# Split-fp32 matmuls of the last stage with weights standing for two of three token groups, and four places where operands, evictions, stores and loads change engine or order

## The chip, the cores and the metric

The kernel runs on one core of one Trainium2 chip. The metric is the device time of one launch in microseconds (us); 829.38 is the median of three runs of the kernel before (828.85 to 832.74). TensorE (PE) multiplies, VectorE (DVE) and ScalarE (ACT) do elementwise work, GpSimd (POOL) does a little of it and issues the accumulating transfers, SyncE (SP) issues all other transfers.

## The reference

Windowed causal attention, a gated layer with SiLU, and a second, ungated pair of layers, all in fp32 on 2304 tokens of width 512:

```
attention: B=4, H=8, S=576, D=64, window 64, softmax, then heads side by side -> x [2304, 512]
moe:  x = (silu(x @ w_gate) * (x @ w_val)) @ w_out          512 -> 1536 -> 512
moe2: out = ((x @ w1) * (x @ w2)) @ w3 @ w_out2             512 -> 1024 -> 1024 -> 512
```

## The kernel before

**Two words.** Each fp32 operand is held as a high and a low word in the format that TensorE takes. The high word is a rounded copy made by a cast (`cast`, line 218, ScalarE); the low word is the difference (`rest`, line 227, VectorE). A product takes three passes: high by high, high by low, low by high (`PASSES`).

**Seven products.** Every large product is a 2x2 block product with seven multiplications instead of eight (`PRODUCTS = (1, 2, 5, 6, 7, 4, 3)`). For the moving tokens this needs, besides the raw blocks, sums and differences of them (`combine`, line 231). An operand of product p and contraction block m has a name that ends in `pm`: `hf0_42` is the operand of product 4, block 2, of token group 0.

**Two ways to a low word.** Normally VectorE subtracts. In a few cases ScalarE writes the negated high word and an accumulating transfer of POOL's queue adds the source to it (`gather`, lines 234 to 236). Line 358 is that ScalarE instruction for the first gated stage; `RESTS` says for which products of which token group this is done there.

**Stages.** Tokens run in three groups of 768 (`TP`), each as two halves of 384 (`T`). Attention comes first and fills other engines' time with the first operands. Then come the first gated stage (`gated`, matmuls at line 666, results added up at lines 678 to 693, h stored by SP at line 756), the projection back to width 512 (`project`, line 830, evicted by ScalarE for one token half and VectorE for the other), the second gated stage with the same function, and the final part (`final`). In the final part w3 @ w_out2 is first multiplied into one matrix w34 (`row`, line 988, out of tiles z and w3T that SP loads at lines 862 and 874). Then the three token groups are multiplied with it (`Group`, line 1008, matmuls at line 1054). `begin` puts the loads of z and w3T into the plan during the second gated stage.

**The last stage before.** The tokens stand: a 128 x 128 piece of the operand hf is the weight, 256 columns of w34 move. A product is 3 pieces of 128 tokens x 4 blocks x 3 passes = 36 matmuls for each half of the tokens of a group, so 7 x 36 = 252 in a group. Results lie in PSUM with tokens on partitions. ScalarE copies 128 x 256 (line 1024), VectorE adds 128 x 256 (line 1028), SP stores rows of 512 or 256 columns (line 1034).

**What sets the order.** A planner at build time (`Plan`, lines 92 to 164) keeps a list of jobs with an assumed cost for every engine and hands them out as its own clock goes on (`advance`). `need` forces a job out directly before the instruction that uses it. On the chip each engine runs its instructions strictly in the order so fixed: an instruction that waits holds all behind it on its engine.

Of the kernel before, what the change touches and what calls it, by code (L numbers as in the profile page):

```python
# [37 lines left out]
def window_attention_moe_kernel(ctx: ExitStack, tc: tile.TileContext, q, k, v, w_gate, w_val, w_out, w1, w2, w3, w_out2, out):  # L38
# [286 lines left out]
    class Operands:  # L325
# [2 lines left out]

        def __init__(self, x, name, after=None, by_dma=(), rest_by_dma=(), due=0.0):
            self.ops, self.jobs = {}, {}

            at = {1: (0, 0), 2: (1, 0), 5: (0, 0), 6: (0, 0), 7: (0, 1), 4: (1, 0), 3: (1, 1)}
            sums = {5: ((0, 1), (1,)), 6: ((1, 1), (5,)), 7: ((1, 1), (5,)), 4: ((0, 0), (6, 2))}

            def blk(m, r, c):
                return x[2 * r + m]()[:, T * c:T * c + T]

            last = {}  # L340
            for p in PRODUCTS:
                for m in range(2):
                    wait, when = [after[p]] if after else [], due + AT[p]
# [12 lines left out]
                    if p in rest_by_dma:  # L356
# [278 lines left out]
    def gated(xop, left, order, func, hd, events, apart=0):  # L635


        hs = {}
        behind, xs = [], []

        def later(n, fn):
# [12 lines left out]
        class Unit:  # L654
# [49 lines left out]
            def product(self, p):  # L704
# [19 lines left out]
                elif p == 6:  # L724
                    plan.wait(self.read)
                    self.mm(self.al, 6)
                    self.c12 = self.own(0, 1, "c12")
                    self.copy(self.c12, self.al)
                elif p == 7:
                    plan.wait(self.read)  # L730
                    self.mm(self.al, 7)
                    c22 = self.own(1, 1, "c22")
                    self.copy(c22, self.al)

                    def summed():
                        self.summed = self.add(c22, c22, self.be)
                        if self.x:
                            self.put(1, 1, c22)
                        else:
                            later(2, lambda: self.put(1, 1, c22))  # L740
                    later(1, summed)
                elif p == 4:
                    plan.wait(self.read)
                    self.mm(self.al, 4)
                    self.put(1, 0, self.al)
                elif p == 3:
                    plan.wait(self.summed)
                    self.mm(self.be, 3)
                    self.add(self.c12, self.c12, self.be)
                    if self.x:  # L750
                        self.put(0, 1, self.c12)
                    else:
                        later(2, lambda: self.put(0, 1, self.c12))
                    if self.x:
                        for i, t in enumerate(hs.pop((self.fp, self.tp))):
                            nc.sync.dma_start(out=hd[self.fp, self.tp][:, i, :], in_=t)
# [45 lines left out]
    def project(rows, wos, events):  # L802

        NF, NM = DF // P, DM // P
        for tp in range(NTP):
# [42 lines left out]
    def final(rows):  # L848
# [9 lines left out]
        def queue_z(f):  # L858
            for x in range(2):
                def load(eng, x=x):  # L860
                    zt[f, x] = slot([P, DM], F32R, f"z{f}{'hl'[x]}")
                    eng.dma_start(out=zt[f, x].bitcast(F32), in_=zd[f][:, x, :])
                jobs["z", f, x] = loading(load, (), 1)

        def queue_w3(n):

# [2 lines left out]
            for g in range(0, NI, 3):  # L869
# [6 lines left out]

                def word(x, g=g, k=k):
                    return w3T[i][g // 3][:, x, :k * P]
                a = loading(load, [done[n - 3]] if n > 2 else (), 1)
# [55 lines left out]
        class Left:  # L935


            def __init__(self, tp):
# [17 lines left out]
                for p in PRODUCTS:  # L956
                    for m in range(R):
# [11 lines left out]
                        b = rest(lambda m=m, p=p: self.ops[p, m][:, 1], lambda m=m, p=p: blk(m, *at[p]),  # L969
                                 lambda m=m, p=p: self.ops[p, m][:, 0], [a], T)  # L970
# [25 lines left out]
            plan.slots += 3  # L996

        def begin():
            keep, plan.rank = plan.rank, -1
            queue_w3(0)  # L1000
            queue_w3(1)
            for f in range(NI):
                queue_z(f)
            for n in range(2, NI):
                queue_w3(n)
            plan.rank = keep

        class Group:
# [28 lines left out]
            def product(self, p):  # L1037
# [12 lines left out]
                for t in range(3):  # L1050
# [24 lines left out]
                        self.store(1, t, 0 if self.tp == NTP - 1 else None)  # L1075
                    plan.advance(1.44)

        def run():
            for n in range(NI):
                if n == 3:  # L1080
# [195 lines left out]

    def operands(tp):
        xop1[tp] = Operands([lambda c=c: X[tp, c] for c in range(KC)], f"xo{tp}",
                            {p: written[m] for p, m in WRITTEN[tp].items()} if tp in WRITTEN else None, BY_DMA[tp], RESTS[tp], 14.0 * tp)

    LANDING = {2: 11.2, 3: 8.5, 7: 6.0}
    second = {4: mark(), 8: mark()}
# [96 lines left out]
```

## Time and profile before

| | us |
|---|---|
| median of three runs | 829.38 |
| profiled execution | 830.3 |
| its span in the trace | 828.6 |
| TensorE busy in the span | 815.5 |
| VectorE / ScalarE / GpSimd busy | 633.0 / 455.7 / 78.2 |

The span runs from the first to the last recorded instruction; 1.7 us of the profiled execution lie around it. The granted TensorE clock is at the upper level in the whole span. A busy time is the union of the engine's instructions, so neighbours that overlap in a pipeline are counted once; mean durations are therefore longer than the distance between two starts.

### The profile page before, as it was taken

To read this page: it belongs to the slowest core of one execution; us is meant where nothing else is said; L and a number is where in the kernel's file an instruction comes from. 1 tells how busy PE (TensorE), PEld (TensorE's weight loads), DVE (VectorE), ACT (ScalarE), POOL (GpSimd) and SP (SyncE) were. 2 spreads that over 40 slices of the span, in tenths; PEclk is the share of its full clock that TensorE was granted. 3 is DMA by queue.
4 is the path that set the end of the run, shared out by engine and by line. 5 is a ranking of instruction groups with operands and counts; after the bars stand their busy time and mean duration, and the time that the engine had idled before them with its cause. 6 is when DMAs were issued, how large, how long until landed. Compare 5 with 4: busy or idle time off the path is not lost.

```text
span 828.6 us, 15847 instructions
## 1 busy us (share of the span) xinstructions
PE 815.5 (98%) x5870; PEld 785.8 (95%) x5870; DVE 633.0 (76%) x1347; ACT 455.7 (55%) x1202; POOL 78.2 (9%) x111
## 2 busy tenths in 40 slices
PE   7999999999999999999999999999999999999998
PEld 5878899999999999999999999999999998899998
DVE  5899989686887949765897683877888744798883
ACT  6999987555555545633553552444344432656452
POOL 3666833000000000000000000000000000000000
PEclk9999999999999999999999999999999999999999
DMA  9998286253562345599987712123565249533422
GB/s 185 212 196 187 45 202 141 90 191 128 191 228 85 134 153 199 210 348 404 352 264 178 237 44 102 39 90 115 166 203 166 86 131 363 171 115 112 157 77 77
DMA packets 150429, 140.24 MB, mean 169 GB/s; under 512 B 95440, under 2 KB 117200, under 8 KB 149328
## 3 DMA queue, kind: packets, MB, share of 16 engines
q1 hardware_dynamic: 147472, 135.29, 52.0%
q0 software_dynamic: 2880, 3.93, 2.9%
q8 instruction: 46, 0.75, 0.4%
q14 instruction: 31, 0.25, 0.1%
HBM read 92.27 MB, written 42.99 MB: 163 GB/s over the span
## 4 chain that ended last, share of the span: by engine, by line
PE 88%; DMA 6%; DVE 2%; ACT 2%; issue 1%; SPq 1%; POOL 0%; ACTq 0%; DVEq 0%
PE ala L666 15%; PE alb L666 15%; PE o L830 14%; PE bea L666 7%; PE beb L666 7%; PE al L1054 6%; PE acc L988 5%; PE gaa L666 4%; PE gab L666 4%; PE be L1054 3%; PE PV L518 2%; DMA zd<-by_z 2%; DMA rawq<-in_q_dram 2%; PE PT L498 2%; PE S L465 2%; PE ga L1054 2%
## 5 line engine op out<-in xcount | busy, mean ns | idle before, releaser
L830 PE MATMUL o<-ph,wo 128*128 128x384 f32 x576 | 146.7, 334 | 0.9 <-DVE X L816 0.7
L830 PEld LDWEIGHTS o<-ph,wo 128*128 128x128 f32 x576 | 103.9, 188 | 1.5 <-DVE X L816 1.0
L830 PE MATMUL o<-pl,wo 128*128 128x384 f32 x288 | 96.2, 334 | 0.0
L376 ACT ACTIVATE ha<-ala 128x384 f32<-128x384 f32 x102 | 49.6, 489 | 53.1 <-PE ala L666 47.1
L678 DVE TENSOR_TENSOR ha<-ha,bea 128x384 f32<-128x384 f32 x60 | 33.1, 551 | 35.5 <-PE bea L666 21.2
L830 PEld LDWEIGHTS o<-pl,wo 128*128 128x128 f32 x288 | 54.1, 188 | 0.0
L479 ACT ACTIVATE pexp<-S,stat 128x128 f32<-128x128 f32 x144 | 52.9, 417 | 0.0
L227 DVE TENSOR_TENSOR hf<-h,hf 128x384 fp32r<-128x384 f32 x84 | 43.5, 552 | 5.7 <-ACT hf L218 5.6
L218 ACT CAST hf<-h 128x384 fp32r<-128x384 f32 x84 | 39.3, 514 | 13.0 <-DVE h L231 11.4
L691 ACT ACTIVATE ha<-ha 128x384 f32<-128x384 f32 x54 | 28.3, 525 | 30.7 <-DVE ha L678 30.7
L218 ACT CAST ph<-pl 128x768 fp32r<-128x768 f32 x36 | 29.0, 836 | 26.9 <-DMA pl<-h 25.7
L227 DVE TENSOR_TENSOR pl<-pl,ph 128x768 fp32r<-128x768 f32 x36 | 33.3, 950 | 12.0 <-ACT ph L218 11.6
L489 POOL TENSOR_TENSOR pexp<-pexp,stat 128x384 f32<-128x384 f32 x48 | 39.0, 833 | 36.3 <-DVE stat L486 20.1
L376 ACT ACTIVATE c12b<-alb 128x384 f32<-128x384 f32 x30 | 14.8, 493 | 47.2 <-PE alb L666 47.1
L479 ACT ACTIVATION_READ_ACCUMULATOR pexp<-S,stat 128x1 f32 x144 | 36.6, 256 | 0.0
L678 DVE TENSOR_TENSOR c22b<-c22b,beb 128x384 f32<-128x384 f32 x30 | 16.6, 553 | 25.0 <-ACT c22b L376 25.0
L472 DVE TENSOR_REDUCE stat<-S 128x3 f32<-128x384 f32 x48 | 24.4, 550 | 8.1 <-PE S L465 7.7
L666 PE MATMUL ala<-xo,w_g_7h 128*128 128x384 f32 x120 | 30.0, 334 | 0.0
L666 PE MATMUL ala<-xo,w_g_1h 128*128 128x384 f32 x126 | 29.2, 335 | 0.0
L1024 ACT COPY o<-al 128x256 f32<-128x256 f32 x36 | 13.4, 373 | 27.0 <-PE al L1054 26.0
L504 DVE COPY ptt<-PT 128x384 f32<-128x384 f32 x48 | 23.8, 537 | 1.8 <-PE PT L498 1.8
L376 ACT ACTIVATE c11b<-alb 128x384 f32<-128x384 f32 x30 | 14.7, 489 | 18.6 <-PE alb L666 18.6
(543 smaller groups left out, 2481.1 us busy)
## 6 DMA issues: line engine op xcount, KB each, us to landing
h<-ha SPq DMA_DIRECT2D x60, 384.0 KB, 3.0
pl<-h SPq DMA_DIRECT2D x36, 384.0 KB, 6.2
h<-h SPq DMA_DIRECT2D x24, 384.0 KB, 4.8
st_w<-in_moe_w_dram SPq DMA_DIRECT2D x8, 1024.0 KB, 6.3
st_wo<-in_moe_w_out_dram SPq DMA_DIRECT2D x6, 1024.0 KB, 5.8
wo<-by_wo SPq DMA_DIRECT2D x12, 512.0 KB, 4.4
st_g<-in_moe_w_gate_dram SPq DMA_DIRECT2D x5, 1024.0 KB, 5.5
st_v<-in_moe_w_val_dram SPq DMA_DIRECT2D x5, 1024.0 KB, 5.5
```

The lines of the kernel that those rows point to most:

```text
L218: (eng.copy if eng is nc.scalar else eng.tensor_copy)(out=hi(), in_=src())
L227: return plan.job(lambda eng: eng.tensor_tensor(out=lo(), in0=src(), in1=hi().bitcast(F32), op=ALU.subtract), after, slots=slots, due=due, ...
L376: nc.scalar.mul(out=out, in_=in_, mul=-1.0)
L472: nc.vector.tensor_reduce(out=st[:, 0, x, :], in_=sc[2 * m + x], op=ALU.max, axis=AX.X, negate=True)
L479: nc.scalar.activation(out=pe[:, jj, :], in_=so[:, jj, :], func=AF.Exp, bias=st[:, 0, x, jj:jj + 1], accum_out=st[:, 1, x, jj:jj + 1])
L489: nc.gpsimd.tensor_tensor(out=pe, in0=pe, in1=st[:, 3, x, :].unsqueeze(2).to_broadcast([P, SUB, P]), op=ALU.mult)
L666: nc.tensor.matmul(acc, lhsT=self.wt.ops[p, x][:, m, :], rhs=self.xs.ops[p, m][:, y, :], start=start and n == 0, stop=n == 5, skip_group_c ...
L678: nc.vector.tensor_tensor(out=out, in0=x, in1=y, op=ALU.add)
L691: nc.scalar.activation(out=h, in_=src, func=func, scale=-1.0 if direct else 1.0)
L830: nc.tensor.matmul(acc[m, x], lhsT=wos.tiles[i // 6][:, i % 6, :], rhs=rows[2 * tp + x].words(f, b), start=f == n == 0, stop=f == NF - 1 a ...
L988: nc.tensor.matmul(acc, lhsT=w3T[i][c // 3][:, x, (c % 3) * P:(c % 3) * P + P], rhs=zt[c, y], start=c == k == 0, stop=c == NI - 1 and k == 2)
L1054: nc.tensor.matmul(acc, lhsT=self.xs.ops[p, m][:, x, t * P:t * P + P], rhs=right.ops[p, m, y], start=start and n == 0, stop=n == 3 * R - 1 ...
```

## The change

Six edits:

1. Token groups 0 and 1 of the last stage are a new class, `Turned`; group 2 stays a `Group`. In `Turned` the pieces of w34 stand (128 of its 256 columns at a time) and 384 tokens move. A product is 2 pieces x 4 blocks x 3 passes = 24 matmuls of 384 columns. Results have features on partitions; VectorE turns them in blocks of 32 x 32 into a tile `ot`, and SP stores each tile with four transfers, one for 32 partitions each, whose runs in memory are 128 bytes. Copies and adds are 128 x 384.
2. In the last stage, for groups 1 and 2, the low words of products 4 and 3 are made by ScalarE's negated copy and an accumulating transfer of POOL's queue.
3. In the first gated stage, token group 1, the low words of product 2 (xo1_20, xo1_21) are subtracted by POOL itself (`aside`), without ScalarE and without a transfer.
4. In the projection, ScalarE evicts both halves of group 1.
5. In the second gated stage, POOL's queue and not SP stores h.
6. The z loads and the first two rows of w3T loads no longer lie freely in the plan but wait for the low word of the last weight's product 3; four z tiles come ahead of the second row of w3T.

The diff, cut to its core:

```
+    def aside(out, x, y, after, due):
+        return plan.job(lambda eng: eng.tensor_tensor(out=out(), in0=x(), in1=y(), op=ALU.subtract), after, due=due, DMA=1.05)
...
+        store = (nc.sync if func != AF.Copy else nc.gpsimd).dma_start
...
-                if x:
+                if x or tp == 1:
...
-                jobs["z", f, x] = loading(load, (), 1)
+                jobs["z", f, x] = loading(load, [left2[max(left2)].jobs[3]], 1)
...
+                        if tp and p in (4, 3):
+                            b = plan.job(lambda eng, m=m, p=p: eng.mul(out=self.ops[p, m][:, 1],
+                                                                       in_=self.ops[p, m][:, 0].bitcast(F32), mul=-1.0),
+                                         [a], ACT=act(T))
+                            b = gather(lambda m=m, p=p: self.ops[p, m][:, 1].bitcast(F32), lambda m=m, p=p: blk(m, *at[p]), [b], 0.0)
...
+        class Turned:
...
+            def store(self, i, c, k, src=None):
+                t = small([P, T], F32, f"ot{self.tp}_{i}{c}{k}")
+                nc.vector.transpose(out=t, in_=self.o[i, c][:, k] if src is None else src)
+                plan.charge("DVE", dve(T))
+                at, col = self.tp * TP + c * T, N2 * i + P * k
+                for a in range(0, P, 32):
+                    nc.sync.dma_start(out=out[at:at + T, col + a:col + a + 32].rearrange("(b p) f -> p b f", p=32),
+                                      in_=t[a:a + 32].rearrange("p (b f) -> p b f", f=32))
...
+                for k in range(2):
+                    acc, n = getattr(self, to)[k], 0
+                    for m in range(R):
+                        for x, y in PASSES:
+                            nc.tensor.matmul(acc, lhsT=right.ops[p, m, y][:, P * k:P * k + P], rhs=self.xs.ops[p, m][:, x, :],
+                                             start=bool(name) and n == 0, stop=n == 3 * R - 1, skip_group_check=not name)
+                            n += 1
...
+                    if kept:
+                        self.copy(*kept, k, acc)
+                    if p == 2:
+                        self.add(0, 0, k, acc)
+                        self.store(0, 0, k)
+                    elif p == 7:
+                        self.add(1, 1, k, self.be[k])
+                        self.store(1, 1, k)
+                    elif p == 4:
+                        self.store(1, 0, k, acc)
...
-                group = Group(tp)
+                group = (Group if tp == NTP - 1 else Turned)(tp)
...
-    RESTS = ((3,), (2, 3), (2, 3))
+    RESTS = ((3,), (3,), (2, 3))
+    ASIDE = ((), (2,), ())
```

**Group 0 on VectorE, from product 7 to product 4.** Here `o0_1x` are output tiles, `be` a bank of PSUM, h2_0_x the raw tokens and hf0_4x the operands of product 4. Before:

```order
L227 TENSOR_TENSOR hf0_40_8739<-h2_0_4_8247,hf0_40_8739 128x384
L231 TENSOR_TENSOR h2_0_6_8265<-h2_0_6_8265,h2_0_2_8259 128x384
L227 TENSOR_TENSOR hf0_41_8761<-h2_0_5_8254,hf0_41_8761 128x384
L1028 TENSOR_TENSOR o0_10_8706<-o0_10_8706,be0_0_8639 128x256
L227 TENSOR_TENSOR hf0_42_8765<-h2_0_6_8265,hf0_42_8765 128x384
L231 TENSOR_TENSOR h2_0_7_8275<-h2_0_7_8275,h2_0_3_8271 128x384
L1028 TENSOR_TENSOR o0_11_8734<-o0_11_8734,be0_1_8640 128x256
L227 TENSOR_TENSOR hf0_33_8604<-h2_0_7_8275,hf0_33_8604 128x384
L227 TENSOR_TENSOR hf0_43_8797<-h2_0_7_8275,hf0_43_8797 128x384
```

After, the same place (line 1110 is the add, line 1115 the turn):

```order
L1110 TENSOR_TENSOR o0_11_8716<-o0_11_8716,be0_0_8615 128x384
L1115 STREAM_TRANSPOSE ot0_110_8731<-o0_11_8716 128x384
L227 TENSOR_TENSOR hf0_40_8711<-h2_0_4_8245,hf0_40_8711 128x384
L227 TENSOR_TENSOR hf0_41_8714<-h2_0_5_8252,hf0_41_8714 128x384
L1110 TENSOR_TENSOR o0_11_8716<-o0_11_8716,be0_1_8616 128x384
L1115 STREAM_TRANSPOSE ot0_111_8755<-o0_11_8716 128x384
L227 TENSOR_TENSOR hf0_42_8737<-h2_0_6_8263,hf0_42_8737 128x384
L231 TENSOR_TENSOR h2_0_7_8273<-h2_0_7_8273,h2_0_3_8269 128x384
L227 TENSOR_TENSOR hf0_43_8763<-h2_0_7_8273,hf0_43_8763 128x384
```

Before, hf0_42 and hf0_43 stand ahead of the adds of the second and the third result of product 7; now both stand behind the add of the second, last result (it reads `o0_11` after ScalarE's copy of `al0_1`) and behind its turn.

**Group 1 on ScalarE, around product 7.** hf1_4x are the operands of product 4; line 1024 and line 1106 are copies of results. Before:

```order
L1024 COPY o1_10_9117<-al1_0_8939 128x256
L218 CAST hf1_40_9126<-h2_1_4_8710 128x384
L218 CAST hf1_41_9131<-h2_1_5_8714 128x384
L218 CAST hf1_42_9136<-h2_1_6_8736 128x384
L1024 COPY o1_11_9150<-al1_1_8940 128x256
L1024 COPY o1_12_9169<-al1_2_8941 128x256
L218 CAST hf1_43_9176<-h2_1_7_8744 128x384
```

After (line 979 is the negated copy that goes ahead of an accumulating transfer):

```order
L218 CAST hf1_40_9050<-h2_1_4_8671 128x384
L1106 COPY o1_01_9016<-al1_1_8886 128x384
L979 ACTIVATE hf1_40_9050<-hf1_40_9050 128x384
L218 CAST hf1_41_9073<-h2_1_5_8679 128x384
L218 CAST hf1_42_9077<-h2_1_6_8688 128x384
L1106 COPY o1_11_9079<-al1_0_8885 128x384
L979 ACTIVATE hf1_41_9073<-hf1_41_9073 128x384
L979 ACTIVATE hf1_42_9077<-hf1_42_9077 128x384
L218 CAST hf1_43_9103<-h2_1_7_8707 128x384
L1106 COPY o1_11_9079<-al1_1_8886 128x384
L979 ACTIVATE hf1_43_9103<-hf1_43_9103 128x384
```

Before, only the casts stood here and VectorE subtracted. Now each operand has an instruction more on ScalarE; those of hf1_41 and hf1_42 stand behind the copy of product 7's first result, that of hf1_43 behind the copy of its second and last one, and behind each a transfer on POOL's queue follows.

**The loads of z on SP, end of the second gated stage.** Before, h2 stores stood among them:

```order
L862 DMA z4h_7970<-zd_4_121 128x512
L862 DMA z4l_7972<-zd_4_121 128x512
L756 DMA h2_3_1_103<-ha3_1_0_7704 128x768
L756 DMA h2_3_1_103<-ha3_1_1_7705 128x768
L862 DMA z5h_7991<-zd_5_122 128x512
L862 DMA z5l_7993<-zd_5_122 128x512
L862 DMA z6h_7995<-zd_6_123 128x512
L862 DMA z6l_7997<-zd_6_123 128x512
L862 DMA z7h_8009<-zd_7_124 128x512
L862 DMA z7l_8011<-zd_7_124 128x512
```

After, no store is left in this queue and the w3T row follows directly:

```order
L871 DMA z6h_7991<-zd_6_123 128x512
L871 DMA z6l_8003<-zd_6_123 128x512
L871 DMA z7h_8005<-zd_7_124 128x512
L871 DMA z7l_8017<-zd_7_124 128x512
L883 DMA w3T1_0_8019<-w3d_125 128x3x128
L883 DMA w3T1_3_8030<-w3d_125 128x3x128
```

The two stores (line 756) have gone to POOL's queue; z7l stands behind loads only.

## Rows read from the trace of the kernel before

**Rows 1.** Page, part 1: busy us and share by engine.

```profile
PE 815.5 (98%) x5870; PEld 785.8 (95%) x5870; DVE 633.0 (76%) x1347; ACT 455.7 (55%) x1202; POOL 78.2 (9%) x111
```

**Rows 2.** The waits, engine PE: who waited for whom, us, times, longest.

```profile
PE gaa L666 <- DMA xo<-X: 1.4, 1, 1.4
PE o L830 <- DVE X L816: 0.7, 1, 0.7
...
PE beb L666 <- DVE w_b_3h L227: 0.5, 1, 0.5
...
PE acc L988 <- DMA z7l<-zd: 0.2, 1, 0.2
```

**Rows 3.** Group 0 of the last stage: stretch; PE, PEld, DVE, ACT, POOL busy; clock, DMA.

```profile
734.37:764.61 30.24, 30.24 (x255) 30.24 (x254) 24.76 (x55) 19.65 (x49) 0.00 (x0) 1.00 0.41 142
```

**Rows 4.** The chain of waits, last stage and gated stage: start us, us, what.

```profile
655.97 1.04 PE bea L666 x6
...
734.37 4.31 PE al L1054 x36
```

**Rows 5.** Timeline (start, us, what, idle before): ScalarE and VectorE, product 7 of group 0.

```profile
753.12 0.37 ACT L1024 COPY o<-al 128x256 f32<-128x256 f32 x1 [0.24 <-PE al L1054]
...
753.53 0.42 DVE L1028 TENSOR_TENSOR o<-o,be 128x256 f32<-128x256 f32 x1 [0.47 <-ACT o L1024]
...
755.31 1.02 DVE L227 TENSOR_TENSOR hf<-h,hf 128x384 fp32r<-128x384 f32 x2
```

**Rows 6.** Groups by form: busy, mean ns; line 1134: ns min/median/max.

```profile
L376 ACT ACTIVATE ha<-ala 128x384 f32<-128x384 f32 x102 | 49.6, 489 | 53.1 <-PE ala L666 47.1 <-PE alb L666 5.2
L227 DVE TENSOR_TENSOR hf<-h,hf 128x384 fp32r<-128x384 f32 x84 | 43.5, 552 | 5.7 <-ACT hf L218 5.6
L218 ACT CAST hf<-h 128x384 fp32r<-128x384 f32 x84 | 39.3, 514 | 13.0 <-DVE h L231 11.4 <-issue 1.6
...
L1134 DVE STREAM_TRANSPOSE by_w<-st_w x16: 662/703/707, 413.7 to 628.9; 128x512 f32<-128x512 f32 x16
```

**Rows 7.** Timeline, VectorE, around operand 6 of the first gated stage.

```profile
115.32 0.56 DVE L678 TENSOR_TENSOR ha<-ha,gaa 128x384 f32<-128x384 f32 x1 [0.23 <-PE gaa L666]
115.80 1.49 DVE L227 TENSOR_TENSOR xo<-X,xo 128x384 fp32r<-128x384 f32 x3
```

**Rows 8.** The chain of waits around the wait for operand 2.

```profile
110.84 0.43 ACT xo L358
...
111.56 3.07 DMA xo<-X
...
114.67 0.44 PE gaa L666
```

**Rows 9.** Timeline, TensorE, the same wait and the next use of an operand.

```profile
112.98 0.34 PE L666 MATMUL gaa<-xo,w_g_1h 128*128 128x384 f32 x1
...
116.19 1.00 PE L666 MATMUL ala<-xo,w_g_4h 128*128 128x384 f32 x4
```

**Rows 10.** The DMA view: KB each, median us to landing.

```profile
X<-X POOLq DMA_DIRECT2D x10, 192.0 KB, 5.0
xo<-X POOLq DMA_DIRECT2D x10, 192.0 KB, 4.1
```

**Rows 11.** Timeline, TensorE, around the load z7l.

```profile
694.83 0.49 PE L988 MATMUL acc<-z7h,w3T 128*128 128x512 f32 x1
695.55 0.50 PE L988 MATMUL acc<-z7l,w3T 128*128 128x512 f32 x1 [0.22 <-DMA z7l<-zd]
695.88 0.40 PE L988 MATMUL acc<-z7h,w3T 128*128 128x512 f32 x1
```

**Rows 12.** Timeline, SyncE, the same loads and the stores among them.

```profile
684.85 0.96 SPq L756 DMA_DIRECT2D h<-ha  x2
...
689.76 0.38 SPq L862 DMA_DIRECT2D z7l<-zd  x1
```

**Rows 13.** Timeline, TensorE, the evictions' wait in the projection.

```profile
415.45 0.45 PE L830 MATMUL o<-ph,wo 128*128 128x384 f32 x1 [0.70 <-DVE X L816]
```

More of the change, by code (lines that the diff above doesn't have):

```diff
@@ L325, in window_attention_moe_kernel, with __init__ @@
     class Operands:
-        def __init__(self, x, name, after=None, by_dma=(), rest_by_dma=(), due=0.0):
+        def __init__(self, x, name, after=None, by_dma=(), rest_by_dma=(), rest_aside=(), due=0.0):
             self.ops, self.jobs = {}, {}
@@ L355, in __init__ @@
                     hi, lo = lambda m=m, p=p: self.ops[p, m][:, 0], lambda m=m, p=p: self.ops[p, m][:, 1]
-                    if p in rest_by_dma:
+                    if p in rest_aside:
+                        b = aside(lo, lambda m=m, p=p: blk(m, *at[p]), lambda hi=hi: hi().bitcast(F32), [a], when)
+                    elif p in rest_by_dma:
                         b = plan.job(lambda eng, hi=hi, lo=lo: eng.mul(out=lo(), in_=hi().bitcast(F32), mul=-1.0),
@@ L878, in word @@
                     return w3T[i][g // 3][:, x, :k * P]
-                a = loading(load, [done[n - 3]] if n > 2 else (), 1)
+                a = loading(load, [done[n - 3]] if n > 2 else [left2[max(left2)].jobs[3]], 1)
                 b = cast(lambda word=word: word(0), lambda word=word: word(1).bitcast(F32), [a], k * P, 0)
@@ L968, in __init__ @@
                         a = cast(hi, lambda m=m, p=p: blk(m, *at[p]), wait, T)
-                        b = rest(lambda m=m, p=p: self.ops[p, m][:, 1], lambda m=m, p=p: blk(m, *at[p]),
-                                 lambda m=m, p=p: self.ops[p, m][:, 0], [a], T)
+                        if tp and p in (4, 3):
[3 more added lines that the diff above has]
+                            b = gather(lambda m=m, p=p: self.ops[p, m][:, 1].bitcast(F32), lambda m=m, p=p: blk(m, *at[p]), [b], 0.0)
+                        else:
+                            b = rest(lambda m=m, p=p: self.ops[p, m][:, 1], lambda m=m, p=p: blk(m, *at[p]),
+                                     lambda m=m, p=p: self.ops[p, m][:, 0], [a], T)
                         last[p, m] = [a, b] if p != 5 else [a, b, wait[0]]
@@ L1000, in begin @@
             queue_w3(0)
-            queue_w3(1)
             for f in range(NI):
                 queue_z(f)
+                if f == 3:
+                    queue_w3(1)
             for n in range(2, NI):
@@ L1076, in product, with __init__, keep, copy @@
                     plan.advance(1.44)
+        class Turned:
+            def __init__(self, tp):
+                self.tp, self.xs = tp, left[tp]
+                self.o = {}
+            def keep(self, i, c):
+                self.o[i, c] = slot([P, 2, T], F32, f"o{self.tp}_{i}{c}")
+            def copy(self, i, c, k, src):
+                nc.scalar.copy(out=self.o[i, c][:, k], in_=src)
+                plan.charge("ACT", act(T))
+            def add(self, i, c, k, src):
+                nc.vector.tensor_tensor(out=self.o[i, c][:, k], in0=self.o[i, c][:, k], in1=src, op=ALU.add)
+                plan.charge("DVE", dve(T))
+            def store(self, i, c, k, src=None):
+                t = small([P, T], F32, f"ot{self.tp}_{i}{c}{k}")
+                nc.vector.transpose(out=t, in_=self.o[i, c][:, k] if src is None else src)
+                plan.charge("DVE", dve(T))
+                at, col = self.tp * TP + c * T, N2 * i + P * k
+                for a in range(0, P, 32):
+                    nc.sync.dma_start(out=out[at:at + T, col + a:col + a + 32].rearrange("(b p) f -> p b f", p=32),
+                                      in_=t[a:a + 32].rearrange("p (b f) -> p b f", f=32))
+                plan.slots += k if src is None else 0
+            def product(self, p):
+                for m in range(R):
+                    plan.need(right.jobs[p, m])
+                    plan.need(self.xs.jobs[p, m])
+                name = {1: "al", 2: "ga", 5: "be"}.get(p)
+                if name:
+                    setattr(self, name, [bank(f"{name}{self.tp}_{k}")[:, :T] for k in range(2)])
+                to = {2: "ga", 5: "be", 3: "be"}.get(p, "al")
+                kept = {1: (0, 0), 6: (0, 1), 7: (1, 1)}.get(p)
+                if kept:
+                    self.keep(*kept)
+                for k in range(2):
+                    acc, n = getattr(self, to)[k], 0
+                    for m in range(R):
+                        for x, y in PASSES:
+                            nc.tensor.matmul(acc, lhsT=right.ops[p, m, y][:, P * k:P * k + P], rhs=self.xs.ops[p, m][:, x, :],
+                                             start=bool(name) and n == 0, stop=n == 3 * R - 1, skip_group_check=not name)
+                            n += 1
+                    if k == 1:
+                        plan.slots += R
+                    if kept:
+                        self.copy(*kept, k, acc)
[7 more added lines that the diff above has]
+                        self.store(1, 0, k, acc)
+                    elif p == 3:
+                        self.add(0, 1, k, acc)
+                        self.store(0, 1, k)
+                    plan.advance(2.08)
@@ L1278, in operands @@
         xop1[tp] = Operands([lambda c=c: X[tp, c] for c in range(KC)], f"xo{tp}",
-                            {p: written[m] for p, m in WRITTEN[tp].items()} if tp in WRITTEN else None, BY_DMA[tp], RESTS[tp], 14.0 * tp)
+                            {p: written[m] for p, m in WRITTEN[tp].items()} if tp in WRITTEN else None, BY_DMA[tp], RESTS[tp], ASIDE[tp], 14.0 * tp)
     LANDING = {2: 11.2, 3: 8.5, 7: 6.0}
```

2 lines of the change are left out of this document (1 added, 1 removed).

## The prediction

> **What bounds the kernel now.** I read the shares of the page first: TensorE is busy 815.5 us of a span of 828.6 [rows 1], so what counts is the time between two matmuls, and any wait that TensorE gets. The list of TensorE's waits comes second; beyond the start of attention it has four that the change could touch [rows 2]. Third, the table by stretch: in token group 0 of the last stage TensorE is busy 30.24 us of 30.24 while VectorE has 24.76 and ScalarE 19.65 [rows 3]. There is no idle time to win there, only fewer or shorter matmuls, and VectorE is the engine with the least room. Last, the timeline around product 7, where TensorE hands results to the engines that also make its next operands [rows 5].
>
> **Edit 1, pace.** A product of 36 matmuls of 256 columns takes 4.31 us, 120 ns each; six of 384 columns take 1.04 us, 173.3 ns each [rows 4]. A group is 252 x 120 ns = 30.24 us before and 168 x 173.3 ns = 29.12 us after. That is 1.12 us less, for two groups 2.24 us less. The columns are the same in number (9216 a product); what goes is the fixed part of 84 matmuls.
>
> [...]
>
> **Edit 1, what is late in group 0.** Count from the group's start, with products 4.16 us apart: product 7 begins at 16.64, its second half ends at 20.80, and product 4 begins there. Before, the low words of product 4's blocks 2 and 3 stood ahead of the last results of product 7 on VectorE, and block 3's was finished at 755.31 + 1.02 = 756.33 [rows 5], just after product 4 began at 755.97 (group start 734.37 [rows 4] + 21.60) and before TensorE needed it. After, both stand behind an add that waits for product 7's last result. A copy starts 0.03 us after the last matmul: 753.12 against 734.37 + 17.28 + 1.44 = 753.09; the add starts 0.04 us after the copy's end [rows 5]. A copy of 384 takes 0.49, a cast 0.51, an operation of VectorE 0.55; the turn of 384 is an estimate from the one of 512, 0.70 x 384/512 = 0.53 [rows 6]. So:
> - copy 20.83 to 21.32; add 21.36 to 21.91; turn 21.91 to 22.44. The next independent operation follows 0.48 us after a start [rows 7]: low word of block 2 from 22.39 to 22.94.
> - TensorE needs that word as the third pass of block 2, at 20.80 + 8 x 0.173 = 22.19, and gets it at 22.98: 0.8 us lost.
> - Block 3's difference follows at 22.87 to 23.42, its cast to 23.97; TensorE is there at 23.16 and waits until 24.01: 0.85. The low word runs to 24.56; TensorE is there at 24.36: 0.24.
>
> Together 1.9 us. If the turn took only 0.35 and the copy 0.37, as 256 columns do, 1.6; with the turn at the 0.70 of 512 columns, 2.1.
>
> **Edit 2, what is late in groups 1 and 2.** Here product 4's low words take a negated copy on ScalarE and an accumulating transfer. In the trace the transfer starts 0.28 us after that copy's end (110.84 + 0.43 to 111.56), takes 3.07 and TensorE goes on 0.04 later [rows 8]. The median of such transfers is 4.1, for the longer kind 5.0 [rows 10]. In group 1 ScalarE does the copy of product 7's first result (18.75 to 19.15, start to start 0.4), the negated copies of blocks 1 and 2, a cast, the copy of the last result (from 20.83) and the negated copy of block 3 (21.23 to 21.76). Its transfer starts at 22.04 and lands at 25.11 with 3.07, at 26.14 with 4.1. TensorE needs it at 20.80 + 11 x 0.173 = 22.71. Block 1's lands at 23.0 where 21.67 is needed, so the loss comes in pieces; all of it together is 25.15 - 22.71 = 2.4 us, or 3.5 with 4.1. Group 2 is a `Group` as before, a third of it 1.44 us, product 4 from 21.60. Its negated copies of blocks 2 and 3 stand only behind the copy of product 7's first third (18.75); block 3's runs 19.44 to 19.97, its transfer starts at 20.25 and lands at 23.32. Needed at 21.60 + 11 x 0.12 = 22.92: 0.4 us lost, with 4.1 it is 1.5. I take 3.6 us for a transfer, halfway, since they come in pairs on one queue and the next group's eight loads of tokens run beside group 1's: 2.9 and 1.0.
>
> The Trainium skill (DMA: Bandwidth & Descriptors, section Anatomy of one DMA) gives a transfer of this queue about 2.0 us plus its bytes over 436 GB/s, for 192 KB an estimate of 2.45 us. The shortest on the chain here is 3.07. By the page the two losses would be 1.8 us and nothing, and the sum +0.6, which stays in the range.
>
> Product 3's words are made long before their use, and loads and results are needed late: nothing for them. The output's 64 small transfers go behind each other on SP and hold only the next loads; these start some 4 us later than the turn of product 2 and have ten more.
>
> **Edit 3.** TensorE lost about 1.5 us at operand 2, block 1 (112.98 to 114.67, less a matmul) [rows 9]. POOL's subtraction ends that. But the next operand is VectorE's: its low word begins at 115.80, behind an add that started at 115.32 after waiting 0.23 us for TensorE itself [rows 7]. Without the wait it begins at 115.57 and is done at 116.12, while TensorE, at that product at 116.19 before [rows 9], would be there at 114.7 and need it at 115.0. So 1.1 of the 1.5 us come back: gain 0.3, at most 1.5, at least nothing.
>
> **Edit 6 with 5.** At z7l TensorE lost 695.55 - 694.83 - 0.23 = 0.5 us, and 0.1 at the next [rows 11]. The load was issued at 689.76, behind stores that waited for VectorE [rows 12]. After, nothing waits for results in that queue: gain 0.6, at worst nothing. The stores in POOL's queue hold only their tiles; POOL has nothing else there. Bound: from nothing to the 2 us by which 5.0 exceeds 3.07; I take nothing, since the tiles are not the next to be written. The 0.5 us for w_b_3h [rows 2] stay: its subtraction still follows an add that waits for TensorE.
>
> **Edit 4.** The only wait for an eviction by VectorE is at 415.45 [rows 13], when TensorE takes the banks of group 0 again; group 1's evictions are changed, and there no wait is named [rows 2]. Nothing; and eight copies of 0.49 us on an engine busy 55% of the span (455.7 us) [rows 1] cost nothing either.
>
> **Sum.** -2.24 - 0.3 - 0.6 + 1.9 + 2.9 + 1.0 = +2.7 us. The profiled execution (830.3) would be 833.0; it lies 0.9 above the median of 829.38, which becomes 832.1. With transfers of 3.07 it is +1.6, with 4.1 +3.8; with the most favourable terms throughout (2.24 + 1.5 + 0.6 against 1.6 + 2.4 + 0.4) it is zero.
>
> **Rivals.**
> - Slow transfers at product 4 of groups 1 and 2. From 4.3 us a transfer the sum passes 4.1 us; at 5.0 [rows 10] the losses are 4.4 and 2.4, the sum +5.6, the time 835.0. For it: loads of 384 KB and output pieces are on their way in group 1. Against: the transfer that the chain shows took 3.07.
> - The stalls don't come, because the operands' engines run ahead of what I assume, and the pace stands alone: -3.1 us, 826.3, and 825.1 if operand 2's wait goes whole. For it: VectorE has 5 us to spare in a group [rows 3]. Against: an order in which the operand follows the result of the product just before it can't be run ahead of.
> - Columns alone count: a matmul of 384 takes 1.5 x 120 = 180 ns in this stage and the pace gains nothing, +4.9, 834.3. For it: so far no row shows w34 standing. Against: the gated stage's six in 1.04 us [rows 4] are of the same shape, 128 x 128 standing and 384 moving. [...]
>
> **Chances.** My sum 0.57 (0.06 of it beyond 4.1 us), slow transfers 0.24, no stalls 0.13 (0.05 of it below -4.1), columns alone 0.05, unseen 0.01. About 0.5%, 4.1 us, is what a measurement tells from no change. Slower by more: 0.06 + 0.24 + 0.05 = 0.35. Faster by more: 0.05 + 0.01 = 0.06. Within: 0.59. The range takes in both sides until about 0.1 is left on each: 827 to 837; the likeliest case's own is 829.4 to 834.
>
> **What would show it.** In the profile after: products of 4.16 us in the first two groups' chain; TensorE waits at the matmuls of product 4 for VectorE's low word and ScalarE's cast in group 0 and for accumulating transfers in groups 1 and 2, of 1.9, 2.9 and 1.0 us; no wait for z7l; a wait of about 1 us for an operand of VectorE where the first gated stage waited for a transfer. Groups of 29.1 us with no wait at product 4 would prove me wrong, and so would waits elsewhere in the last stage.

## The result and the profile after

| | before | after |
|---|---|---|
| median of 6 runs each, side by side | 829.95 us (828.85 to 832.74) | 839.69 us (838.98 to 842.90) |
| ratio | | 1.0118, 95% interval 1.0102 to 1.0133 |
| profiled execution: time, span | 830.3, 828.6 us | 838.98, 837.3 us |

The changed kernel is 1.2% slower, 9.7 us by the medians. The forecast was 832.1 us with a range to 837: the sign was right, the predicted difference of 2.7 us too small by a factor of more than three, and the time lies outside the range. What follows finds the 7 us that were missed.

I read the shares of the page first (busy us, share of the span, instructions). They answer to [rows 1]:

```profile
PE 817.1 (98%) x5702; PEld 785.0 (94%) x5702; DVE 632.0 (75%) x1337; ACT 461.1 (55%) x1208; POOL 105.5 (13%) x151
```

TensorE has 168 matmuls fewer, as two groups of 84 should give, and 1.6 us more busy time, part of it at a lower clock, as shown below. Of the 8.7 us by which the span grew, 7.1 lie in the gaps between matmuls. Next the waits of TensorE (who waited for whom: us in total, times, longest), against [rows 2]:

```profile
PE al L1138 <- DMA hf<-h: 3.8, 1, 3.8
...
PE ala L674 <- DVE xo L227: 2.1, 3, 1.2
...
PE T L434 <- DVE w_g_2l L227: 1.4, 1, 1.4
PE al L1071 <- DMA hf<-h: 1.4, 2, 0.8
PE al L1138 <- DVE hf L227: 0.8, 1, 0.8
PE beb L674 <- DVE w_b_3h L227: 0.6, 1, 0.6
PE al L1138 <- ACT hf L218: 0.6, 1, 0.6
```

L1138 is the matmul of the turned products, L1071 that of the third group. The waits for operand 2 (gaa) and for z7l are gone from the list. In their place stand waits before product 4, in all three groups, and a new one for VectorE in the gated stage (L674), 2.1 us in three pieces. The 1.4 us at L434 is in attention, where both kernels run the same instructions in the same order: chance of the one profiled execution.

Third, the table by group of the last stage (us; busy PE, PEld, DVE, ACT, POOL with instructions; granted clock, DMA share, GB/s), for [rows 3] and the two groups behind it:

```profile
735.49:766.81 31.32, 29.99 (x169) 29.01 (x169) 26.07 (x56) 18.87 (x45) 2.46 (x4) 1.00 0.51 140
766.81:801.87 35.06, 31.22 (x171) 29.95 (x170) 25.01 (x52) 17.94 (x41) 7.17 (x9) 0.95 0.93 196
801.87:837.30 35.43, 30.74 (x253) 30.13 (x251) 17.61 (x39) 13.71 (x33) 4.35 (x5) 0.99 0.37 85
```

Before, the same three stretches are (same columns):

```profile
764.61:794.85 30.24, 30.24 (x254) 30.24 (x254) 24.46 (x52) 16.32 (x40) 0.00 (x0) 1.00 0.47 157
794.85:828.60 33.75, 30.23 (x252) 30.03 (x251) 20.58 (x44) 10.84 (x26) 0.00 (x0) 0.99 0.17 62
```

with group 0 in [rows 3]. The account of the two profiled executions closes: the last stage starts 1.12 us later (735.49 for 734.37), group 0 is 1.08 longer, group 1 4.82, group 2 1.68; together 8.70, the difference of the spans. More than half of it is group 1. The DMA share there is 0.93; before it was 0.47.

The chain of waits shows the pace, against [rows 4] (start us, us, what):

```profile
739.67 4.16 PE ga L1138 x24
...
786.77 6.16 DMA hf<-h
792.93 0.04 issue
792.98 4.73 PE al L1138 x19
...
822.29 4.09 DMA hf<-h
```

24 matmuls take 4.16 us, as predicted. The two transfers in the chain take 6.16 and 4.09 us; the prediction gave both 3.6.

### The profile page after: what moved, and what is told of

Same layout as the page of the kernel before. It is cut to its first block, busy times and chain, and to the rows that moved or that the text cites. A ratio compares the mean times of both kernels' runs of the same rounds, so it can differ in the third digit from the quotient of the medians.

```text
span 837.3 us, 15603 instructions
## 1 busy us (share of the span) xinstructions
PE 817.1 (98%) x5702; PEld 785.0 (94%) x5702; DVE 632.0 (75%) x1337; ACT 461.1 (55%) x1208; POOL 105.5 (13%) x151
## 4 chain that ended last, share of the span: by engine, by line
PE 85%; DVE 4%; DMA 4%; issue 4%; ACT 2%; POOL 0%; SPq 0%; POOLq 0%; DVEq 0%; ACTq 0%
PE o L839 18%; PE ala L674 14%; PE alb L674 13%; PE bea L674 7%; PE beb L674 7%; PE acc L1003 5%; PE gaa L674 4%; PE gab L674 3%; PE al L1138 3%; PE PV L524 2%; PE S L471 2%; PE PT L504 2%; PE T L434 2%; PE be L1138 1%; DMA hf<-h 1%
## 5 line engine op out<-in xcount | busy, mean ns | idle before, releaser
L764 POOL DMA_DIRECT2D h<-ha x24 | 12.9, 544 | 549.4 <-DVE ha L696 549.4
L495 POOL TENSOR_TENSOR pexp<-pexp,stat 128x384 f32<-128x384 f32 x48 | 39.0, 833 | 38.2 <-DVE stat L492 30.5
L227 DVE TENSOR_TENSOR hf<-h,hf 128x384 fp32r<-128x384 f32 x68 | 34.4, 547 | 2.8 <-ACT hf L218 2.8
L674 PE MATMUL ala<-xo,w_g_7h 128*128 128x384 f32 x120 | 29.8, 335 | 0.0
L674 PE MATMUL ala<-xo,w_g_1h 128*128 128x384 f32 x126 | 29.2, 335 | 0.0
L236 POOL DMA_DIRECT2D hf<-h x16 | 14.0, 988 | 113.7 <-ACT hf L979 85.8
```

The costliest lines, as they stand in the source:

```text
L227: return plan.job(lambda eng: eng.tensor_tensor(out=lo(), in0=src(), in1=hi().bitcast(F32), op=ALU.subtract), after, slots=slots, due=due, ...
L495: nc.gpsimd.tensor_tensor(out=pe, in0=pe, in1=st[:, 3, x, :].unsqueeze(2).to_broadcast([P, SUB, P]), op=ALU.mult)
L674: nc.tensor.matmul(acc, lhsT=self.wt.ops[p, x][:, m, :], rhs=self.xs.ops[p, m][:, y, :], start=start and n == 0, stop=n == 5, skip_group_c ...
```

## The experiments

Ten kernels beside the change. Each time stands beside the kernel before on the same chip (its median there: 830.54 for the first four, 830.07 for the next four, 830.48 for the last two). The changed kernel was not measured again there: a difference to its 839.69 is one of medians from two sets of runs, and where the difference of the ratios says something else, it is given.

**Without the transfers for the low words.**

```
-                        if tp and p in (4, 3):
+                        if False:
```

> The changed kernel without edit 2: VectorE makes the low words of products 4 and 3 in groups 1 and 2 as before. Theory (the transfers' landing is what group 1 and 2 lose by): the TensorE waits for hf transfers go; what stays is VectorE's order, 1.9 us in group 0 and about 1.4 in group 1, whose block 3 still stands behind product 7's last add and turn; some 6 us less than the changed kernel's 839.7, so 833 to 835. Rival (the turns alone make VectorE too full, the transfers only relieved it): new VectorE waits of 3 us or more in groups 1 and 2, 837 or more.

Measured: 833.35 us, ratio 1.0037 (1.0024 to 1.0050), 6.3 us under the changed kernel. Groups 0 and 1 last 31.32 and 30.89 us, the third has no wait for a transfer. So edit 2 carries about two thirds of the loss.

**Without the subtraction on GpSimd.**

```
-    RESTS = ((3,), (3,), (2, 3))
-    ASIDE = ((), (2,), ())
+    RESTS = ((3,), (2, 3), (2, 3))
+    ASIDE = ((), (), ())
```

> The changed kernel without edit 3: operand 2 of token group 1 in the first gated stage by ScalarE and a transfer again. Theory (POOL's subtraction slows VectorE's subtractions beside it from 0.55 to 1.37 us, and TensorE waits for these): xo0_40 and xo0_41 take 0.55 us again, the two TensorE waits of about 0.6 us before operand 2 and the one of 1.2 behind it go, the transfer's wait of 1.4 comes back; TensorE is 1 to 1.5 us earlier by the middle of that stage, of which up to 1 is lost again at the projection's evictions: 0.3 to 1.5 us less than 839.7. Rival (the two long subtractions of VectorE are chance of the one profile): no difference at that place.

Measured: 837.81 us, ratio 1.0090 (1.0071 to 1.0109), 1.9 us under the changed kernel (2.3 by the ratios, whose intervals touch; each of its four executions, 836.77 to 838.80, lies under the six of the changed kernel). The 1.4 us wait for operand 2 is back, and the kernel is faster with it.

**Long runs in the output.** The stores of the turned tiles write runs of 1536 bytes; there are as many stores as before. They go to places in the output that are not theirs: the kernel leaves out the output's order.

```
-                    nc.sync.dma_start(out=out[at:at + T, col + a:col + a + 32].rearrange("(b p) f -> p b f", p=32),
-                                      in_=t[a:a + 32].rearrange("p (b f) -> p b f", f=32))
+                    nc.sync.dma_start(out=region[a:a + 32], in_=t[a:a + 32])
```

> The changed kernel with the turned tiles stored in runs of 1536 bytes, as many transfers and bytes, to places in the output that are not theirs (the output's order is left out). Theory (the loads of group 2's tokens, 3 MB issued just before, delay group 1's accumulating transfers): landings in group 1 stay at 5 to 7 us, the wait stays above 4.5 us, time within 1.5 us of 839.7. Rival (the 128-byte pieces delay them): landings of 3 to 4.5 us, group 1 loses 2.5 to 3.5 us, time 836 to 837.5.

Measured: 839.61 us against 839.69, ratio 1.0101 (1.0078 to 1.0124). The transfers of group 1 land after 6.8, 6.2, 6.7 and 6.4 us. The 128-byte pieces of the output are not what slows them; whether they cost a microsecond elsewhere, the interval leaves open.

**Product 7's adds and turns behind product 4's operands.**

```
+                if p == 4:
+                    for k in range(2):
+                        self.add(1, 1, k, self.be[k])
+                        self.store(1, 1, k)
...
-                    elif p == 7:
-                        self.add(1, 1, k, self.be[k])
-                        self.store(1, 1, k)
```

> The changed kernel with product 7's adds and turns issued behind the operands of product 4 instead of ahead. Theory (group 0 loses by the place of two low words on VectorE): the waits for VectorE's hf and ScalarE's hf of group 0, 1.9 us, shrink to under 0.5, group 1 and 2 keep theirs, which wait for transfers: 838. Rival (VectorE is simply behind by then): the wait stays within 0.5 us of 1.9.

Measured: 844.36 us, ratio 1.0160 (1.0133 to 1.0186): 4.7 us slower than the changed kernel (3.5 by the ratios), where up to 2 us faster was expected. Group 0 did what was expected, 29.15 us without a wait. But the order moved the rest: in group 1 the loads now end at 794.60 and the four transfers, issued from 786.22 on, take 7.4 to 8.3 us; in group 2 each of ScalarE's negated copies comes behind a copy of one of product 7's results, so that the last transfer is issued 22.7 us after the group's start for 20.4. The edit was not the single cut that I took it for, and alone it cannot show what the order on VectorE costs. TensorE's clock adds to it (group 1, columns as above):

```profile
766.12:804.64 38.52, 32.08 (x170) 30.66 (x170) 24.75 (x50) 18.84 (x42) 7.99 (x10) 0.91 0.93 190
```

**All three at once: no transfers, no subtraction on GpSimd, adds and turns deferred.** The three edits shown above, together.

> The changed kernel with three of its parts undone or mended together: product 4's and 3's low words of the last stage by VectorE again, as in the kernel before (no accumulating transfers there); no subtraction on GpSimd; and product 7's second additions and turns queued behind the making of product 4's operands. What stays is the turned products, their pace, and the reordered loads. Theory (the price of the change is the transfers beside the loads, the subtraction on GpSimd and product 7's VectorE work in front of hf0_4x; the gain of turning is there): the last stage gains 2.2 us of pace and loses at most 0.5 in waits, the stage before gains the 0.6 us of the z tile, so 827 to 828.5 us, about 0.3% under the kernel before, and groups 0 and 1 of the last stage last 29.1 to 29.6 us each. Rival (VectorE has no room left: by the rows before it is busy 24.8 of 30.2 us in a group, and turning adds its turns): groups 0 and 1 last 30.5 us or more with waits for DVE, and the time is 830 us or more.

Measured, in five rounds: 828.35 us, ratio 0.9978 (0.9964 to 0.9992). Faster than the kernel before, by about 1.8 us, and 11.3 us faster than the change. Groups 0 and 1:

```profile
735.79:764.93 29.14, 29.14 (x170) 29.14 (x169) 24.49 (x53) 17.20 (x41) 0.00 (x0) 1.00 0.48 136
764.93:794.19 29.26, 29.26 (x171) 29.09 (x170) 27.25 (x57) 15.28 (x34) 0.00 (x0) 1.00 0.65 166
```

That is the predicted pace of 29.12 without a stall worth naming. VectorE, at 27.25 of 29.26 us, still had room; the rival falls.

**The same with product 3's words by transfers.**

```
-                        if tp and p in (4, 3):
+                        if tp and p == 3:
```

> As the run with all three parts undone or mended, but product 3's low words in groups 1 and 2 of the last stage are made by accumulating transfers; product 3 comes last in its group, so these have about 4 us more before TensorE wants them. Theory (a transfer costs by how late it lands, not by being one): with landings of 6 to 8 us beside the loads of the group after, the words are there 0 to 2 us before or after TensorE wants them, so within 1 us of the other run: 827 to 829 us. Rival (any transfer in this place is too slow): TensorE waits 2 us or more for product 3 in group 1, and the time is 830 us or more.

Measured: 828.22 us, ratio 0.9974 (0.9957 to 0.9990), no wait for them. Here accumulating transfers cost nothing that can be measured, since their words are wanted late enough.

**Group 2's tokens asked for later.**

```
-                    if p == 6 and tp + 1 < NTP:
+                    if p == (6 if tp == 0 else 4) and tp + 1 < NTP:
```

> The changed kernel whole, but group 2's tokens are asked for at product 4 of group 1 instead of product 6, so that their eight loads of 384 KB are issued after the four accumulating transfers of hf1_4x and not before them. Theory (these loads delay the transfers): hf1_4x lands in 3 to 4.5 us after issue (6.2 to 7.0 in the changed kernel), and TensorE's wait before product 4 of group 1 falls from 4.7 to 2 to 3.2 us; what it gains may be lost again at the start of group 2, where the tokens then come later, by up to several us. Rival (the transfers are slow by themselves in this place, or by the stores): they still take 5.5 us or more and the wait stays at 4 us or more.

Measured, in one round of two executions: 850.96 us, ratio 1.0245 (1.0220 to 1.0270). The DMA view of the moment in which hf1_4x are issued (KB each, median us to landing), first the changed kernel, 784 to 790 us:

```profile
hf<-h POOLq DMA_DIRECT2D x4, 192.0 KB, 6.4
```

and with the loads behind them, 783 to 789 us:

```profile
hf<-h POOLq DMA_DIRECT2D x4, 192.0 KB, 4.2
```

They land after 3.5, 3.9, 4.5 and 4.7 us, the last of them 0.2 over the expected window, and TensorE's waits before product 4 add up to 3.2 us in four pieces, where the changed kernel has 3.8 in one. The loads slow the transfers. The group was no shorter for it (34.9 us): after these waits TensorE's granted clock was low for 3.6 us, which gave the gain back (busy columns, clock and DMA share as above):

```profile
792.70:796.30 3.60, 3.53 (x12) 3.53 (x13) 0.58 (x1) 0.00 (x0) 0.00 (x0) 0.54 0.35 60
```

And the tokens of group 2 came late: TensorE waited for them at its start, and the whole is 11 us slower than the changed kernel.

**No turned products.** The kernel before with edits 4 to 6 alone. Edits 2 and 3 are undone as shown above, and edit 1 so:

```
-                group = (Group if tp == NTP - 1 else Turned)(tp)
+                group = Group(tp)
```

> The kernel before with the reordered loads and waits alone (the z and w3 loads, the h stores, the other engine for one eviction): no turned products, no transfers for the low words, no subtraction on GpSimd. Theory: the 0.6 us wait for the z tile goes and little else changes: 0 to 0.8 us under the kernel before. Against the run with all three parts mended it shows what turning alone is worth: about 2.2 us by the pace (24 matmuls in 4.16 us for 4.31). Rival (turning gives nothing once VectorE carries it): the two runs within 0.5 us of each other.

Measured: 830.23 us, ratio 0.9990 (0.9974 to 1.0005). The edits 4 to 6 are worth less than can be told here. Turning alone, against the run with all three mended: 1.9 us by the medians, 1.0 by the ratios, whose intervals overlap; the lengths of groups 0 and 1 show it better, 2.08 (30.24 + 30.24 less 29.14 + 29.26).

**The subtraction on GpSimd alone, in the kernel before.** The hunks of edit 3 and nothing else.

```
+                    if p in rest_aside:
+                        b = aside(lo, lambda m=m, p=p: blk(m, *at[p]), lambda hi=hi: hi().bitcast(F32), [a], when)
...
+    RESTS = ((3,), (3,), (2, 3))
+    ASIDE = ((), (2,), ())
```

> The kernel before with one part of the change alone: the eight subtractions that make product 2's low words of xo1 go to GpSimd instead of VectorE. Theory (GpSimd's and VectorE's subtractions slow each other where they meet): xo1_20 and xo1_21 take 1.3 to 1.4 us on GpSimd, the VectorE subtractions beside them 1.3 to 1.4 for 0.55, TensorE's wait at gaa goes and others of more than its 1.4 us come, so 1.3 to 2.5 us over the kernel before, about 831.5 to 832.5. Rival (the prediction: the wait goes and nothing takes its place): 0.3 to 1.4 us under the kernel before.

Measured, in five rounds: 831.89 us, ratio 1.0019 (1.0009 to 1.0028), 1.4 us over the kernel before (0.7 to 2.3 by the interval). The theory holds, the gain that was predicted isn't there. The expectation counts eight subtractions; there are two, one for each block.

**The order on VectorE by itself.** The change without edits 2 and 3, adds and turns not deferred.

> The changed kernel without the transfers for the low words of the last stage and without the subtraction on GpSimd, with product 7's additions and turns where the change has them, ahead of product 4's operands on VectorE. Against the run that queues them behind it shows what this order costs by itself. Theory: groups 0 and 1 of the last stage last about 31.3 and 30.9 us, TensorE waits 1.3 to 1.9 us before product 4 in each, and the time is 3 to 4 us over that run: 831 to 832.5 us, no longer below the kernel before. Rival (the order is free once the transfers are gone): within 1 us of that run, 828 to 829.5.

Measured: 832.99 us, ratio 1.0026 (1.0013 to 1.0039), 4.6 us over the run that defers them (4.0 by the ratios); 3 to 4 were expected, and 831 to 832.5 us. Group 1 lasts 30.90 us as expected, group 0 32.91 for the 31.3 expected. The timeline of TensorE in group 0 (start, us, what, idle before it and who ended that) shows the same two waits as the changed kernel, and what came after:

```profile
754.27 0.45 PE L1138 MATMUL al<-hf,w_22h 128*128 128x384 f32 x1 [0.76 <-DVE hf L227]
755.28 0.44 PE L1138 MATMUL al<-hf,w_43h 128*128 128x384 f32 x1 [0.56 <-ACT hf L218]
755.56 0.34 PE L1138 MATMUL al<-hf,w_63l 128*128 128x384 f32 x1
...
756.24 0.53 PE L1138 MATMUL al<-hf,w_70h 128*128 128x384 f32 x1
756.56 0.53 PE L1138 MATMUL al<-hf,w_60l 128*128 128x384 f32 x1
```

From 755.87 to 759.44 the matmuls stand 0.32 us apart, 384 columns at 1.2 GHz, and not 0.173. The table by stretch of the same kernel (columns as above) has the granted clock:

```profile
754.00:755.80 1.80, 0.97 (x3) 0.48 (x3) 1.22 (x3) 1.08 (x3) 0.00 (x0) 1.00 0.77 139
755.80:759.40 3.60, 3.60 (x12) 3.53 (x12) 2.91 (x7) 3.60 (x10) 0.00 (x0) 0.53 0.52 89
759.40:764.14 4.74, 4.74 (x28) 4.74 (x28) 3.54 (x7) 0.79 (x2) 0.00 (x0) 1.00 0.32 53
```

Eleven matmuls at 0.147 us more make 1.6 us, which is what group 0 is too long. In the run without transfers, with the same two waits at 759.42 and 760.43, the clock stayed at full speed:

```profile
761.00:764.50 3.50, 3.50 (x21) 3.47 (x21) 2.99 (x7) 3.50 (x10) 0.00 (x0) 1.00 0.31 52
```

Six kernels keep this order and have the same two waits in group 0. In two of them, this one and the one with long runs, the clock fell behind the waits, and the group lasts 32.9 us; in the other four it stayed, and the group lasts 31.3. The same stretch with long runs:

```profile
759.00:762.00 3.00, 3.00 (x12) 3.00 (x11) 2.87 (x6) 3.00 (x8) 0.00 (x0) 0.51 0.22 53
```

So waits of less than a microsecond are sometimes followed by a stretch at half speed and sometimes not. Which of the two an execution gets is open.

## Why the prediction was wrong

**Held.** The pace: 24 matmuls in 4.16 us, 2.08 us gained in two groups where nothing stalls, for the 2.24 predicted. The rival "columns alone count" falls with it. The stall of group 0 at product 4: 2.2 us (31.32 less 29.12) for 1.9, at the two places named. VectorE's and ScalarE's timeline, against [rows 5], has the steps of the walk:

```profile
756.35 0.48 ACT L1106 COPY o<-al 128x384 f32<-128x384 f32 x1 [1.19 <-PE al L1138]
756.86 0.55 DVE L1110 TENSOR_TENSOR o<-o,be 128x384 f32<-128x384 f32 x1
757.45 0.58 DVE L1115 STREAM_TRANSPOSE ot<-o 128x384 f32<-128x384 f32 x1
757.95 0.52 DVE L227 TENSOR_TENSOR hf<-h,hf 128x384 fp32r<-128x384 f32 x1
...
758.97 3.41 ACT L218 CAST hf<-h 128x384 fp32r<-128x384 f32 x8 [2.14 <-DVE h L231]
759.51 0.56 DVE L227 TENSOR_TENSOR hf<-h,hf 128x384 fp32r<-128x384 f32 x1 [0.58 <-ACT hf L218]
```

The turn of 384 took 0.58 for the estimate of 0.53. That this is the cause is shown by the runs that defer the adds: 29.14 and 29.15 us. Group 2 came out 1.68 longer for 1.0; its transfers took 3.0, 3.6, 3.2 and 4.1 us, and with the last of these the prediction's own working gives 1.5. The wait for z7l went, 0.6 us by the profile. The h stores in GpSimd's queue landed in 3.2 us (median of 24) and hurt nothing.

**The step that failed: "I take 3.6 us for a transfer".** The walk to it was right to a hundredth: the transfer of group 1's last block was to start 22.04 us after the group did, at 788.85, and it did. Of its landing only the 3.6 us were wrong: it took 6.2, the four of them 7.0, 6.2, 6.6 and 6.2. TensorE needed the word at 789.52 and took it at 795.17, 5.65 us late for 2.9. GpSimd's issue of that transfer (timeline, start, us):

```profile
788.85 0.86 POOL L236 DMA_DIRECT2D hf<-h  x1 [0.34 <-ACT hf L979]
```

and TensorE at the first and at the last of the four words:

```profile
791.73 0.53 PE L1138 MATMUL al<-hf,w_70h 128*128 128x384 f32 x1 [3.77 <-DMA hf<-h]
...
795.17 0.46 PE L1138 MATMUL al<-hf,w_43h 128*128 128x384 f32 x1
```

The reason stood in the prediction as a half sentence ("the next group's eight loads of tokens run beside group 1's"), and with the order in pairs it was given half a microsecond, 3.6 for 3.07. The loads are eight of 384 KB, issued from 778.31 on; the last is issued at 781.8 and lands after 9.1 us, at 790.9. SyncE's timeline of their issue:

```profile
778.31 4.01 SPq L954 DMA_DIRECT2D h<-h  x8
```

and the DMA view of the last one, from 781.9 us on:

```profile
h<-h SPq DMA_DIRECT2D x1, 384.0 KB, 9.1
```

When the first of the four transfers was issued, at 784.69, five of the loads, 1.9 MB, had not landed. No transfer landed before the last load did; then they came at 791.7, 792.9, 794.0 and 795.0, about a microsecond apart, so by the landings the later ones waited for those ahead of them in their queue as well. This was the rival "slow transfers"; it was priced from the longest median of the old trace, 5.0 [rows 10], and those transfers ran beside other traffic than this. Their spread was on view in the old trace, where all of line 236 has (DMA to landing, us):

```profile
DMA to landing us min/median/max: 3.0/4.7/8.7
```

That the loads are the cause and not the output's pieces is shown by two runs: with the loads behind the transfers the median falls from 6.4 to 4.2, with long runs in the output it stays.

**The second: "POOL's subtraction ends that", gain 0.3.** The edit costs 1.4 us alone and about 1.9 in the changed kernel. The wait for operand 2 ended, and the next one, for VectorE's word, came with 1.21 us for the 1.1 predicted. What was not foreseen stands ahead of both. VectorE in the changed kernel around the new subtraction (timeline, start, us):

```profile
108.39 0.56 DVE L696 TENSOR_TENSOR ha<-ha,c11b 128x384 f32<-128x384 f32 x1
108.87 2.65 DVE L227 TENSOR_TENSOR xo<-X,xo 128x384 fp32r<-128x384 f32 x2
```

GpSimd at the same time:

```profile
108.45 2.65 POOL L240 TENSOR_TENSOR xo<-X,xo 128x384 fp32r<-128x384 f32 x2 [4.43 <-ACT xo L218]
```

and the same two subtractions of VectorE without the edit:

```profile
108.04 1.02 DVE L227 TENSOR_TENSOR xo<-X,xo 128x384 fp32r<-128x384 f32 x2
```

2.65 us for 1.02: each takes 1.37 for 0.55, and GpSimd's two 1.37 and 1.32. TensorE, which wants just these words of VectorE, waits twice, 0.35 and 0.49 us after the end of the matmul before:

```profile
110.29 0.44 PE L674 MATMUL ala<-xo,w_g_4h 128*128 128x384 f32 x1 [0.35 <-DVE xo L227]
...
111.57 0.45 PE L674 MATMUL ala<-xo,w_g_4h 128*128 128x384 f32 x1 [0.49 <-DVE xo L227]
...
118.78 1.16 PE L674 MATMUL ala<-xo,w_g_4h 128*128 128x384 f32 x5 [1.21 <-DVE xo L227]
```

It has lost 1.4 us before operand 2 is even due (2.69 behind the kernel before at that place, 1.30 of it since attention). No trace has this subtraction on GpSimd by itself; its multiplication of the same size in attention takes 0.83 (L495 in the page of groups, x48), and 0.83 and 0.55 make 1.38. So the lengths are those of two engines that take turns: whoever comes second waits out the other's instruction. The prediction had costed GpSimd's time as free.

The Trainium skill (SBUF — State Buffer, section Who interferes with whom) states that a VectorE instruction with two inputs in SBUF contends with a GpSimd instruction that reads SBUF, and calls the port pair that they share an exclusive lock. The trace agrees, with the 1.37 us above. By that rule an estimate with the 0.83 puts the two words 2 x 0.83 us later and the term at +1.4 (1.66 less 0.3), which is what the run of edit 3 alone measured.

**Without weight.** Edit 4: the wait of [rows 13] is absent in the changed kernel, but 0.3 to 0.6 us of it are there in four runs that keep the edit; it follows the landing of a weight load that took 7.3 to 8.8 us from run to run, and I read it as chance.

**The sum by terms** (profiled executions, predicted and then found): pace -2.24, -2.1; edit 3 -0.3, +1.4 to 1.9; edits 5 and 6 -0.6, -0.6; group 0's stall +1.9, +2.2; group 1's +2.9, +5.9; group 2's +1.0, +1.7. The found ones add up to 8.5 to 9.0 for the 8.7 between the spans. Some 3 us were missed in group 1, 2 in edit 3, 1 in the rest; the profile of after lies another 1.3 behind by the end of attention, by chance, and won 1.4 back in the projection, 1.0 of it at the wait of [rows 13].

In the changed kernel the clock too fell in group 1, to 0.58 from 792 to 796 us, after the wait of 3.77. There it cost next to nothing, since the landings of the other three words (792.93, 794.00, 795.02) set the pace until it had risen again.

## What to carry to other kernels

A transfer that a matmul waits for is priced by what else is in flight at that time, not by the median of its kind: add up the bytes that have not landed when it is issued, and the transfers ahead of it in its own queue, and ask when those land. Work moved to an "idle" engine is free only if it doesn't slow the engine that it relieves, as the 1.37 us for 0.55 did here; look at what the relieved engine does at that moment. And of a change in several parts, undo them one by one: here the pace won 2 us and the rest lost over 10, and the parts worth keeping made a kernel of 828.35 us, 0.2% under the one before.

## What the runs showed of the hardware that was not expected

- A subtraction of 128 x 384 on VectorE takes 1.37 us for 0.55 while GpSimd subtracts beside it, and GpSimd's 1.32 to 1.37. In the same place without GpSimd: 0.55.
- TensorE's granted clock fell to the 1.2 GHz level for some 3.5 us after waits that were short: after 0.76 and 0.56 us in one kernel, after waits of 0.3 to 1.6 us in another. The cost, 1.6 us in the first, is there more than the waits themselves, and it doesn't come each time: after the same two waits of group 0 the clock fell in two of six kernels.
- Runs of 128 bytes or of 1536 in 64 stores of 48 KB made no difference that could be measured (839.69 and 839.61 us; ratios 1.0118 and 1.0101 with intervals that overlap).
